# Keeping split tiles and split weights in DRAM between two attention layers

## The chip, the cores and the metric

The kernel runs on one core of one Trainium2 chip. A core has five engines that run side by side and meet through semaphores: TensorE (PE, matmuls), VectorE (DVE), ScalarE (ACT), GpSimd (POOL) and SyncE (SP). SP does no arithmetic here: it issues the transfers (DMAs) between DRAM and the core's own memory, in the order of its instructions. If one of them has to wait, all behind it wait too. The metric is the device time of one execution in microseconds (us). Less is better.

## What is computed

The input `x` has 2048 rows (positions) of 640 numbers, in float32. Four layers follow one another, each with a layer normalization ahead of it and added to its own input:

```
x = x + A(layernorm(x), wqkv, wo)                 # attention
x = x + B(layernorm(x), dft_seq, dft_hid)         # FNet mixing
x = x + A(layernorm(x), wqkv, wo)                 # the same weights again
x = x + B(layernorm(x), dft_seq, dft_hid)         # the same matrices again

A: qkv = x @ wqkv; 32 heads of 20; each position attends to 8 positions,
   itself and those 2, 4, ... 14 before it; softmax; result @ wo
B: a = x @ dft_hid_re.T;  b = x @ dft_hid_im.T
   y = dft_seq_re @ a - dft_seq_im @ b
```

Both attention layers use the same `wqkv`, and both FNet layers the same sequence matrices. What is prepared from them in one layer can therefore be used in another.

## The kernel before

A float32 product is made of three matmuls in a reduced format. An operand is split into a high part (a rounded copy, made by ACT) and a low part (what is left, a subtraction made by DVE or POOL). The matmuls are high by high, high by low and low by high (`PASSES`, L210). "Split" means this pair from here on. A split tile takes twice the room of the raw one.

The work is four calls: `layer_a(0)`, the FNet layer `b1`, `layer_a(2)`, the FNet layer `b2`.

**The attention layers** (`layer_a`) follow a list written out by hand. The function `at(step, phase, ...)` puts a call into a step, from −7 to 66, and a phase of that step; the phases of a step run in the order of `PHASES` (L806), among them `dma` near the beginning and `dmaw`, `dmas`, `misc`, `dmac`, `dmar` near the end. Every engine, SP included, gets its instructions in that order. The work has three strands:

- PE makes the query, key and value products (`qkv_mm`, L344, 64 groups of 15 matmuls). Quarter `q` of the heads uses the split weights `wq[q]`, which live in the buffer `r1_q`. ACT copies each group out, and SP stores it to DRAM (`kvb`, `qb`).
- DVE and POOL do the attention itself, in 32 units of two half steps. SP loads a unit's queries (`q_load`) and its windows of keys and values (`w_load`, L399, in five buffers `win`). DVE multiplies (L423, L461), POOL and DVE sum (L425, L431, L476 to L478), ACT does the exponential (L439) and copies the queries (L396).
- PE makes the output product (`wo_mm`, L501) and, in the last third (steps 49 to 66 and a tail), already begins the FNet layer: `z_mm` (L916) multiplies the normalized rows by the first of eight sequence tiles, in 16 pieces `s` of 128 by 512. These pieces are the tile c0.

In the first attention layer c0 comes raw: `c_load` (L881) loads a piece, `c_hi` (L885) and `c_lo` (L900) split it into a buffer `ct[s]`. In the second, `c_get` (L890) loads a piece that is already split, from the DRAM buffer `c0b`, into the same three (at the end four) buffers in turn:

```
tag = ("s3", "s0", "s2", "s1")[s % (3 if s < 12 else 4)]
```

**The FNet layers** (`LayerB`) take the other sequence tiles in pairs (`pair`, L1091). PE's order in them is written by hand; for the other engines a scheduler orders the instructions by a simulated timeline. A pair has three loops over eight pieces; in the second one (L1159 to L1173), in the first FNet layer and for pairs 0 and 1 alone, the line

```
if self.li == 1 and p < 2:
    self.c_keep(p * NP + i, views, tags)
```

loads one more raw piece of c0, splits it and stores both parts to `c0b`. This is how `c0b` is filled before the second attention layer reads it. The products of `zt` with the DFT weights, which lead to `y`, are at L994 (`ymm`). They come at fixed places of each pair and serve as marks in time.

**The join.** The last pair of the first FNet layer runs inside `early()` (L565) of the second attention layer, with hooks that begin the attention layer's transposes. At hook 7 `w0` loads and splits the weights of quarter 0; quarters 1 to 3 follow after the pair. `a_weights_q` (L204) does this for five pieces of a quarter: a raw piece into a `win` buffer, then ACT (L123) and DVE (L127) split it into `r1_q`. In the first attention layer the weights are split elsewhere (`wq_split`, L540), in the first few steps.

## Time and profile before

| | us |
|---|---|
| runs shown (three): median | 1813.44 |
| lowest and highest | 1812.18, 1818.15 |
| the profiled execution | 1810.4 |
| its span, first to last instruction | 1808.5 |
| PE busy, of the span | 1746.1 |
| mean granted TensorE clock | 0.992 |

The rows of the profile give an engine's busy time, the number and the mean length of a group of instructions, and behind a bar how long the engine stood idle ahead of them and what ended that. "L354" is line 354 of the kernel. PEld is the loading of weights into TensorE, which runs beside the matmuls. A row of the order in time has the start and the length in us. "SPq" marks an instruction of SP that issues a DMA; the name `win<-kvb` means that `win` is written from `kvb`. A matmul's end is modelled, so a PE that is shown busy may still be short of its peak. In the windows view, each row is a stretch of the span, with the busy time of PE, PEld, DVE, ACT and POOL, then the granted clock, the mean busy share of the 16 DMA engines, and the rate in GB/s.

### The profile page before, as it was taken

The page shows a single profiled execution, that of the slowest core. Times are in us where ns is not written, and L with a number is a line of the kernel's source. Part 1 is how long each engine was busy: PE and PEld are TensorE (multiplying, and loading weights), DVE is VectorE, ACT ScalarE, POOL GpSimd, SP SyncE. Part 2 cuts the span into 40 slices and gives each one's busy share as a digit, 9 for nine tenths or more (in the row PEclk, how much of TensorE's full clock was granted, in tenths as well). Part 3 has the DMA queues.
Part 4 walks back from the last instruction along what each step waited for, and adds up shares of the span by engine and source line. Part 5 has one row for each costly group of instructions (what it writes and reads, how often), then busy time and mean ns, then how long its engine had stood idle before and what let it go on. Part 6 is the DMA issues. An engine that isn't in the chain of part 4 may idle for free.

```text
span 1808.5 us, 26471 instructions
## 1 busy us (share of the span) xinstructions
PE 1746.1 (97%) x8798; PEld 1508.9 (83%) x8798; DVE 1380.1 (76%) x2129; ACT 818.9 (45%) x1708; POOL 640.6 (35%) x597
## 2 busy tenths in 40 slices
PE   9999997989999999999999999999899999999999
PEld 6879886777887887888888889877788888888888
DVE  5899899888768767767739988887777677676673
ACT  5544544544445445445533334444434443443441
POOL 3799898960000000000008987899400000000000
PEclk9999998999999999999999999999999999999999
DMA  6776667647789689677647856687687766876761
GB/s 233 224 263 208 208 203 247 218 164 280 273 267 332 223 270 336 221 258 229 215 132 226 278 181 199 200 296 261 218 295 257 259 226 225 265 231 223 259 210 52
DMA packets 273738, 423.59 MB, mean 234 GB/s; under 512 B 22688, under 2 KB 152736, under 8 KB 273344
## 3 DMA queue, kind: packets, MB, share of 16 engines
q1 hardware_dynamic: 270400, 419.92, 70.0%
q10 hardware_dynamic: 3200, 1.97, 0.4%
q8 instruction: 70, 1.15, 0.2%
q14 instruction: 68, 0.56, 0.1%
HBM read 336.66 MB, written 85.14 MB: 233 GB/s over the span
## 4 chain that ended last, share of the span: by engine, by line
PE 65%; DVE 12%; DMA 10%; POOL 6%; ACT 3%; issue 3%; SPq 1%; DVEq 0%; ACTq 0%; POOLq 0%
PE m L354 17%; PE aux L994 13%; PE t L1083 9%; PE m L1083 9%; PE xt L1083 4%; PE pq L1083 4%; PE aux L501 4%; DMA win<-cs_in 2%; DVE pr L423 2%; DVE pr L461 2%; PE m L916 2%; PE t L916 2%; POOL pr L476 2%; DMA c0b<-r 2%; DVE r L1077 1%
## 5 line engine op out<-in xcount | busy, mean ns | idle before, releaser
L354 PE MATMUL m<-r,s 128*128 128x480 f32 x1920 | 439.9, 384 | 5.7 <-ACT s L224 2.4
L354 PEld LDWEIGHTS m<-r,s 128*128 128x128 f32 x1920 | 357.5, 189 | 61.5 <-ACT s L224 3.8
L166 POOL TENSOR_TENSOR stats<-stats,mhalf 128x1 f32<-128x1 f32 (+1 forms) x40 | 30.4, 761 | 564.9 <-ACT stats L162 564.8
L1076 ACT CAST r<-win 128x512 fp32r<-128x512 f32 x244 | 149.4, 620 | 178.4 <-DVE win L1112 75.5
L994 PE MATMUL aux<-r2a,zo 128*128 128x320 f32 x768 | 226.5, 310 | 0.0
L476 POOL TENSOR_TENSOR pr<-pr 128x640 f32<-128x640 f32 x126 | 200.9, 1595 | 40.7 <-DVE pr L461 39.7
L423 DVE TENSOR_TENSOR pr<-pq,win 128x1280 f32<-128x1280 f32 x128 | 189.8, 1483 | 29.9 <-ACT pq L396 29.3
L994 PE MATMUL aux<-pr,zo 128*128 128x320 f32 x704 | 208.2, 308 | 0.0
L1077 DVE TENSOR_TENSOR r<-win,r 128x512 fp32r<-128x512 f32 x244 | 164.5, 686 | 46.8 <-ACT r L1076 40.7
L461 DVE TENSOR_TENSOR pr<-pq,win 128x1280 f32<-128x1280 f32 x128 | 190.8, 1491 | 4.5 <-DVE pq L456 0.2
L425 POOL TENSOR_TENSOR pr<-pr 128x640 f32<-128x640 f32 x128 | 183.4, 1433 | 18.7 <-DVE pr L423 15.6
L1083 PE MATMUL m<-r,r 128*128 128x512 f32 x600 | 154.7, 392 | 0.4 <-DVE r L1077 0.4
L994 PEld LDWEIGHTS aux<-r2a,zo 128*128 128x128 f32 x768 | 144.1, 188 | 2.0
L1083 PE MATMUL t<-r,r 128*128 128x512 f32 x498 | 135.4, 393 | 2.5 <-issue 2.5
L916 PE MATMUL m<-s,r 128*128 128x512 f32 x384 | 119.8, 399 | 15.3 <-DMA s<-c0b 6.7
L1083 PEld LDWEIGHTS m<-r,r 128*128 128x128 f32 x600 | 112.4, 188 | 25.8 <-DVE r L1077 0.7
L994 PEld LDWEIGHTS aux<-pr,zo 128*128 128x128 f32 x704 | 132.1, 188 | 2.0
L916 PE MATMUL t<-s,r 128*128 128x512 f32 x384 | 118.4, 395 | 2.3 <-DVE ot L976 1.5
L361 ACT COPY stg<-m 128x480 f32<-128x480 f32 x128 | 70.9, 556 | 104.6 <-PE m L354 94.0
L477 POOL TENSOR_TENSOR pr<-pr 128x320 f32<-128x320 f32 x126 | 114.4, 908 | 9.9
L431 DVE TENSOR_REDUCE lg<-pr 128x64 f32<-128x640 f32 x128 | 103.9, 811 | 17.7 <-POOL pr L425 17.4
L1083 PEld LDWEIGHTS t<-r,r 128*128 128x128 f32 x498 | 93.4, 188 | 24.6 <-issue 3.3
(269 smaller groups left out, 3246.3 us busy)
## 6 DMA issues: line engine op xcount, KB each, us to landing
win<-cs_in SPq DMA_DIRECT2D x358, 256.0 KB, 4.1
r<-xc SPq DMA_DIRECT2D x240, 256.0 KB, 4.3
win<-kvb SPq DMA_DIRECT2D x96, 440.0 KB, 4.8
xa<-cs_in SPq DMA_DIRECT2D x124, 256.0 KB, 4.2
win<-kvb SPq DMA_DIRECT2D x64, 360.0 KB, 5.3
xc<-stg SPq DMA_DIRECT2D x40, 512.0 KB, 3.1
kvb<-stg SPq DMA_DIRECT2D x60, 320.0 KB, 3.9
xr<-xs SPq DMA_DIRECT2D x40, 320.0 KB, 3.2
```

The source lines that it names most:

```text
L354: nc.tensor.matmul(mt[g][:, : 3 * F], st[:, a, k], wq[q][:, b, k], start=n == 0, stop=n == 14)
L423: nc.vector.tensor_tensor(pr, q, wview(u, jp, 0, [[1, FE]]), op=ALU.mult)
L425: nc.gpsimd.tensor_tensor(pv[:, :, 0:10], pv[:, :, 0:10], pv[:, :, 10:20], op=ALU.add)
L431: nc.vector.tensor_reduce(lgs[u][:, 2 * jp : 2 * jp + 2].rearrange("p j w h -> p (j w h)"), prq.pop((u, jp))[:, :, 0:10], axis=AX.X, op=AL ...
L461: nc.vector.tensor_tensor(pr.rearrange("p j w (h d) -> p j w h d", d=DH), lgs[u][:, 2 * jp : 2 * jp + 2].unsqueeze(4).to_broadcast([P, 2, ...
L476: g.tensor_tensor(pr[:, :, 0:4], pr[:, :, 0:4], pr[:, :, 4:8], op=ALU.add)
L477: g.tensor_tensor(pr[:, :, 0:2], pr[:, :, 0:2], pr[:, :, 2:4], op=ALU.add)
L916: self.last = nc.tensor.matmul(self.z[t][k], self.xn[c][:, a, j, k * P : (k + 1) * P], self.ct[s][:, b], start=s == 0 and i == 0, stop=s = ...
L994: self.last = nc.tensor.matmul(self.ym[e][:, :320], zt[(k, a, ri)][:, j2 * P : (j2 + 1) * P], w[:, e * 320 : (e + 1) * 320], start=(k, a, ...
L1076: nc.scalar.copy(hi, raw)
L1077: nc.vector.tensor_tensor(lo, raw, hi.bitcast(F32), op=ALU.subtract)
L1083: nc.tensor.matmul(bank, w(a, kb), hl[b], start=start and (a, b) == (0, 0), stop=stop and (a, b) == (1, 0),)
```

## The change

The first attention layer now stores what it has split anyway. `wq_keep` writes the split weights of quarter `q`, piece `k`, to a new DRAM buffer `wqb`, at step 16 + 4k + q, in the phase `dmar`. `c_keep` now writes `ct[s]` to `c0b` straight from the buffer that the products read, in the step of the piece's first product; pieces 14 and 15 are written in the tail. The FNet layer's `c_keep` calls are gone.

The second attention layer loads the split weights with `wq_get` into `r1_q`: quarter 0 at hook 7, quarter 1 after the pair, quarters 2 and 3 from the list, at steps −5 to −3 and −2 to 0. `a_weights_q` is gone, and with it twenty splits. Its pieces of c0 now go through five buffers: `s3`, `s2`, the two `stg` buffers and `s0`. The first five are loaded in steps 48 to 50, the others one step after the last product of the piece that held the buffer, though no later than the step before their own first product. In the first attention layer the buffers' turn is `s3`, `s2`, `s0` in place of `s3`, `s0`, `s2`.

```diff
+    wqb = dr.tile([P, NQ, KD, 2, 3 * F], F32, name="wqb")
...
-    def a_weights_q(q):
-        wt = T([P, 2, KD, 3 * F], f"r1_{q}", F32R)
-        for k in range(KD):
-            split(wt[:, 0, k], wt[:, 1, k], wq_load1(q, k))
-        return wt
...
+        def wq_keep(q, k):
+            nc.sync.dma_start(wqb[:, q, k], wq[q][:, :, k].bitcast(F32))
+
+        def wq_get(q, k):
+            if k == 0:
+                wq_begin(q)
+            nc.sync.dma_start(wq[q][:, :, k].bitcast(F32), wqb[:, q, k])
...
             def w0():
                 with tc.issue_after(prev.dma.ins):
-                    wq[0] = a_weights_q(0)
+                    for k in range(KD):
+                        wq_get(0, k)
...
-            for q in range(1, NQ):
-                wq[q] = a_weights_q(q)
+            for k in range(KD):
+                wq_get(1, k)
+                at(-5 + k // 2, "dmar", wq_get, 2, k)
+                at(-2 + k // 2, "dmar", wq_get, 3, k)
...
+            for q in range(NQ if first else 0):
+                at(16 + NQ * k + q, "dmar", wq_keep, q, k)
...
                 at(t - 1, "misc", handoff.c_lo, z)
+                at(t, "dmac", handoff.c_keep, z)
+            elif z < 5:
+                at(*((48, "dma"), (48, "dma"), (48, "dmac"), (49, "dma2"), (50, "dmac"))[z], handoff.c_get, z)
             else:
-                at(t - 1, "dmac", handoff.c_get, z)
+                at(max(50, min(thirds[3 * z - 13] + 1, t - 1)), "dma2", handoff.c_get, z)
...
+            at(64, "dmac", handoff.c_keep, 13)
...
                 handoff.c_hl(14)
+                handoff.c_keep(14)
...
                 handoff.c_hl(15)
+                handoff.c_keep(15)
...
-            tag = ("s3", "s0")[s % 2] if t else ("s3", "s0", "s2", "s1")[s % (3 if s < 12 else 4)]
+            tag = ("s3", "s0")[s % 2] if t else ("s3", "s2", "s0", "s1")[s % (3 if s < 12 else 4)]
...
         def c_get(self, s):
-            tag = ("s3", "s0", "s2", "s1")[s % (3 if s < 12 else 4)]
-            self.ct[s] = T([P, 2, 512], tag, F32R)
+            tag = ("s3", "s2", "stg", "stg", "s0")[s % 5]
+            self.ct[s] = T([P, 2, 512], tag, F32R, bufs=2 if tag == "stg" else 1)
             nc.sync.dma_start(self.ct[s].bitcast(F32), c0b[:, s])
 
-        def c_keep(self, s, views, tags):
-            hi, lo = self.s_split(self.s_raw(0, s, tags), views)
-            for a, v in enumerate((hi, lo)):
-                nc.sync.dma_start(c0b[:, s, a].rearrange("p (r t) -> p r t", r=2), v.bitcast(F32))
+        def c_keep(self, s):
+            nc.sync.dma_start(c0b[:, s], self.ct[s].bitcast(F32))
...
-                    if self.li == 1 and p < 2:
-                        self.c_keep(p * NP + i, views, tags)
```

## The prediction

> **What bounds the kernel now.** I read the page first, then windows of engine time by stage, then the waits and single engines in order of time around each place that the diff touches.
>
> ```profile
> span 1808.5 us, 26471 instructions
> PE 1746.1 (97%) x8798; PEld 1508.9 (83%) x8798; DVE 1380.1 (76%) x2129; ACT 818.9 (45%) x1708; POOL 640.6 (35%) x597
> ```
>
> TensorE (PE) is busy for 1746 of 1808 us and no matmul is added or removed, so only its 62 us of idle time, and time at a lowered clock, can be won. The question is which of it the change reaches. The next answer is the windows view (us; busy time of PE, weight load, DVE, ACT, POOL; granted clock; DMA share; GB/s). The windows are four passes of the same code in `pair`: from the first y product of a pair to the second. The chain and the order of time give their bounds (the chain dates a matmul 0.16 us later, at both ends alike).
>
> ```profile
> 520.98 8.82 PE aux L994 x60
> 572.25 8.82 PE aux L994 x60
> 659.25 0.30 PE L994 MATMUL aux<-r2a,zo 128*128 128x320 f32 x1
> ...
> 520.82:572.09 51.27, 48.87 (x229) 40.11 (x228) 33.92 (x54) 24.47 (x44) 0.00 (x0) 1.00 0.93 327
> 659.25:712.40 53.15, 50.23 (x230) 41.30 (x228) 33.42 (x55) 24.95 (x45) 0.00 (x0) 0.97 0.91 316
> 799.55:847.02 47.47, 47.47 (x230) 40.37 (x228) 31.23 (x49) 21.11 (x39) 0.00 (x0) 1.00 0.68 223
> 1416.78:1464.25 47.47, 47.47 (x229) 40.37 (x228) 30.02 (x48) 19.65 (x34) 0.00 (x0) 1.00 0.75 245
> ```
>
> Pairs 0 and 1 of the first FNet layer hold the sixteen old `c_keep` calls (L1173); pair 2 and the second FNet layer have none. Without them the stage takes 47.47 us with PE never idle; with them 51.27 and 53.15. Who waits is in the answers on the line that stores (L898):
>
> ```profile
> L898 SPq DMA_DIRECT2D c0b<-r x22: 359/377/513, 536.2 to 711.8; - x22
> L898 SPq DMA_DIRECT2D c0b<-s x10: 319/327/636, 521.5 to 694.7; - x10
>   ACT r L1076: 12.6, 5
>   ACT s L1076: 7.3, 2
>   DVE r L1077: 5.0, 1
> DMA to landing us min/median/max: 4.5/5.3/6.2
> ```
>
> 32 stores of 256 KB each hold a split buffer for 4.5 to 6.2 us, and ACT and DVE stand still for 24.9 us until stores let go. DMA engines are at 0.91 to 0.93 there, against 0.68 to 0.75 without.
>
> **The change part by part.**
>
> *Pairs 0 and 1 lose the keep.* Sixteen extra loads (256 KB), 32 stores, 16 ACT and 16 DVE splits go. The price is the window difference: (51.27 − 47.47) + (53.15 − 47.47) = 3.80 + 5.68 = 9.48 us. PE is in order and its idle time is gone at 47.47, so what is late next is PE itself, and everything after moves up. Ends: 0 (something else as long turns up) and −9.48. I take −9.5, for two undisturbed passes lie at 47.47 exactly.
>
> *The join into the second attention layer.* Twenty raw weight loads with 20 ACT and 20 DVE splits become twenty loads of split pairs (480 KB).
>
> ```profile
> L123 ACT ACTIVATE r<-win 128x480 fp32r<-128x480 f32 x20 | 11.9, 603 | 4.6 <-DMA win<-wqkv_in 3.5 <-PE m L1083 0.8
> L127 DVE TENSOR_TENSOR r<-win,r 128x480 fp32r<-128x480 f32 x20 | 12.8, 655 | 5.9 <-ACT r L123 5.8
> 875.00:940.00 65.00, 62.87 (x369) 57.74 (x368) 30.94 (x57) 29.49 (x61) 0.00 (x0) 1.00 0.47 147
> 876.26 5.01 SPq L201 DMA_DIRECT2D win<-wqkv_in  x5
> 892.02 1.60 ACT L123 ACTIVATE r<-win 128x480 fp32r<-128x480 f32 x3 [0.78 <-PE m L1083]
> 893.82 3.94 PE L354 MATMUL m<-r,s 128*128 128x480 f32 x17
> 914.70 0.71 PE L354 MATMUL m<-r,s 128*128 128x480 f32 x2 [1.28 <-ACT s L224]
> 916.30 3.09 PE L354 MATMUL m<-r,s 128*128 128x480 f32 x13 [0.57 <-ACT s L224]
> 928.18 3.23 PE m L354 x15
> ```
>
> The splits take 11.9 us of ACT and 12.8 of DVE, but PE idles only 65.00 − 62.87 = 2.13 us in the stretch. The 1.28 us wait for ACT's transposed copy (L224), queued behind splits and statistics, should go; the 0.57 is the turn PE to ACT to PE and mostly stays. I take −1.5. Ends: −2.1 (all idle time), and above if the loads are late. At the stage's 327 GB/s for a share of 0.93, full engines move about 352 GB/s, so 480 KB take 1.4 us. The five loads of quarter 0 are issued near 876 and the first product is at 893.8: five times 1.4 and the 5.3 of a landing end near 888, 5 us early. Quarter 1 needs buffer r1_1, free at about 892 (the row of ACT waiting for PE); ten loads for quarters 1 and 2 are 14 us, in by 911; the first product of quarter 1 is at 928. Quarter 3 is put on SP behind the first attention loads:
>
> ```profile
> 943.53 0.43 SPq L409 DMA_DIRECT2D win<-kvb  x1
> 948.40 1.48 DVE L423 TENSOR_TENSOR pr<-pq,win 128x1280 f32<-128x1280 f32 x1
> win<-kvb SPq DMA_DIRECT2D x96, 440.0 KB, 4.8
> ```
>
> That window has 4.87 us from issue to use and lands in 4.8; two quarter-3 loads ahead of it (2.8 us, issued some 2 us earlier) make it about 1 us late. DVE's next steps wait for PE's evacuations anyway, so I count 0 and keep +1 as the end.
>
> *Tile loads of the second attention layer: five buffers, started earlier.*
>
> ```profile
> PE m L916 <- DMA s<-c0b: 6.7, 4, 2.7
> 1184.00:1287.00 103.00, 91.68 (x484) 78.44 (x484) 88.25 (x135) 44.29 (x112) 97.67 (x90) 0.98 0.81 276
> L476 POOL TENSOR_TENSOR pr<-pr 128x640 f32<-128x640 f32 x19 | 29.8, 1571 | 2.3 <-DVE pr L461 2.3
> 1286.19 0.66 POOL L478 TENSOR_TENSOR zo<-pr 128x160 f32<-128x160 f32 x1
> 1287.64 0.60 PE L319 MATMUL pq<-ident,zo 128*128 128x128 f32 x4
> ```
>
> The waits on c0b are 6.7 us in four places, but POOL is busy for 97.67 of these 103 us. Its last sum ends at 1286.85; the last transposes start at 1287.64, behind it and DVE's sibling sums. A PE that never waits for tiles would wait there instead. Only POOL's 2.3 us of waiting for DVE can move, where DVE waited for a late PE. I take −0.3; ends −2.3 and +1 (2.5 MB of tiles bunched in two steps at a DMA share of 0.81).
>
> *First attention layer: twenty weight stores of 480 KB, steps 16 to 35.*
>
> ```profile
> 119.00:222.00 103.00, 103.00 (x544) 91.86 (x543) 93.18 (x131) 56.58 (x148) 93.67 (x91) 1.00 0.66 210
> 167.21 0.42 SPq L409 DMA_DIRECT2D win<-kvb  x1
> 175.83 1.48 DVE L423 TENSOR_TENSOR pr<-pq,win 128x1280 f32<-128x1280 f32 x1
> ```
>
> 9.8 MB in 103 us are 95 GB/s more: 305 of 352, share 0.66 to about 0.9. They wait for nothing, having been split long before, and SP's issue is some 0.4 us each. Behind them stand the window loads; the pair shown has 8.6 us from issue to use, over 4.8 to land: a store ahead costs 1.4 of 3.8 spare. I take +0.2; ends 0 and +3 (single misses). The Trainium skill, in DMA: Bandwidth & Descriptors, section Bandwidth, measures 425 GB/s for large loads by a core alone and sets about 358 where HBM binds. By the first figure the queue would be at 0.72 and this part free; the trace's 352 says the second, with a sum 0.2 us higher.
>
> *First attention layer's tail: sixteen tile stores of 512 KB, steps 49 to the end, and slots in another order.*
>
> ```profile
> 272.00:387.00 115.00, 97.36 (x493) 83.88 (x491) 103.76 (x155) 53.31 (x128) 105.79 (x94) 0.93 0.68 224
> ACT s L888 <- DMA stg<-cs_in: 17.3, 8, 3.6
> 327.14 0.62 ACT L888 CAST s<-stg 128x512 fp32r<-128x512 f32 x1 [2.31 <-DMA stg<-cs_in]
> 331.10 1.49 DVE L423 TENSOR_TENSOR pr<-pq,win 128x1280 f32<-128x1280 f32 x1 [0.22 <-ACT pq L396]
> 433.18 0.83 DVE L125 SCALAR_TENSOR_TENSOR zo<-xa,zo 128x640 fp32r<-128x640 f32 x1 [0.63 <-ACT zo L123]
> ```
>
> DVE and POOL are busy 104 and 106 of 115 us, so every delay to them counts. A keep waits on SP for DVE's low part of the step before, where SP already waits for windows that DVE frees; behind it in the queue are the raw tile loads, for which ACT waits in order (17.3 us in eight places), and behind ACT the softmax and the query copies. 512 KB at 352 GB/s are 1.5 us. At 327 the delay shows: ACT waits 2.31 us for a tile, and DVE 0.22 for the query copy behind it. I count that place in full (1.5) and half a microsecond for the rest, since elsewhere ACT mostly waits for DVE: +2.0, ends 0 and +6. The last two keeps share the queue with the next layer's DFT weights, whose last split ends at 434.0, just when it is used: +0.3, ends 0 and +2.
>
> Sum: −9.5 − 1.5 − 0.3 + 0.2 + 2.0 + 0.3 = −8.8 us, on the profiled 1810.4 us (span 1808.5): 1801.6. The median of the runs shown, 1813.4, is 3.0 above that profile; against it the sum is about 1804.6. I say 1804.
>
> **Rivals.**
>
> *The tile waits were worth their full time.* If the end of the second attention layer follows PE, 6.7 us go, and the 2.3 above are not the limit: 1804 − 6.4 = 1798. For it: the chain passes through c0b loads. Against: POOL is full.
>
> *The join gives the gain back.* Split loads are twice as large and must wait for the weight buffer itself, where raw tiles waited in window buffers. If quarter 0's loads, on a queue with more ahead of them than I count, lose the 5 us by which they are early and, say, another landing and a load (5.3 + 1.4, some 7 us), PE stands at the first product: 1804 + 7 = 1811. Against: share 0.47.
>
> *Slower: the store queue stalls the first tail.* ACT meets a raw tile 1.5 us late for each of 13 tiles, and nothing absorbs it: 13 × 1.5 = 19.5 in place of 2.0, so 1804 + 17.5 = 1821. The other terms win 10.8 us, so the kernel is slower than before from the eighth uncovered tile on, and by over 0.3% from the eleventh. Against: in the row of that line ACT waits for eight tiles only, and DVE is behind it in one of the rows. A second way to the same stall is the slot, now held until the store has landed (5.3 us), but its next tile comes three tiles later. The Trainium skill, DMA: Bandwidth & Descriptors, section Anatomy of one DMA, says completion waits for the write receipt, HBM's the heaviest, and puts 2.0 us plus bytes over 436 GB/s on a DMA; that would be 3.2 us for 512 KB. The 5.3 measured for half the size speaks for the queue as the larger part.
>
> **How the numbers follow.** Forecast with its terms' ends: 0.72, for its main term stands in two pairs of windows. Full tile waits 0.06, join 0.13, slower 0.09. A change of 0.3% (5.4 us) is about what a measurement of this kernel can tell from none: faster is below 1808.0. So faster 0.78, same 0.13, slower 0.09. The range takes in the forecast's ends and the join, and leaves out the slow case: 1797 to 1811; the likeliest case alone has 1797 to 1808.
>
> **What would show it.** Both stages at 47.5 us with a DMA share near 0.7 and no c0b store; the join without the 1.28 us wait; no c0b waits of PE at the second tail, but POOL's last sum as late after the layer's start as now, and a new short wait of PE for it; in the first tail ACT's waits for raw tiles grown from 17.3 us and that stretch 2 us longer. Wrong would be a first tail longer by over 8 us, PE idle ahead of the first product of the second attention layer, or windows landing after DVE wants them in steps 16 to 35.

## The result, and the profile after

| | us |
|---|---|
| the changed kernel: median of four runs | 1827.2 (1824.6 to 1830.2) |
| the kernel before, beside it on the same chip | 1815.0 (1812.2 to 1818.2) |
| ratio, with its 95% interval | 1.0071 (1.0056 to 1.0086) |
| profiled execution after, its span | 1827.6, 1825.8 |

The change made the kernel slower by 0.7%, some 12 us; the forecast was 1804. In all comparisons below, the runs of the kernel before lay between 1810.3 and 1820.8 us, so its profile (1810.4) is one of its quickest executions. Differences between the two profiles (17.3 us of span) are therefore some 5 us larger than those between medians. Places and waits are read from the profiles, verdicts from the runs.

The head of the page after:

```profile
span 1825.8 us, 26342 instructions
PE 1755.1 (96%) x8798; PEld 1519.0 (83%) x8798; DVE 1371.7 (75%) x2093; ACT 800.8 (44%) x1672; POOL 641.1 (35%) x597
```

ACT and DVE have less to do (800.8 against 818.9, 1371.7 against 1380.1), as the splits are gone, and yet the span is longer. The windows view of the changed kernel shows where (columns as in the prediction: the stretch, busy time of PE, PEld, DVE, ACT, POOL, granted clock, DMA share, GB/s):

```profile
119.00:222.00 103.00, 103.00 (x543) 91.77 (x543) 93.08 (x131) 56.91 (x148) 93.61 (x91) 1.00 0.92 300
272.00:387.00 115.00, 92.28 (x473) 79.52 (x471) 103.56 (x146) 49.63 (x119) 101.65 (x90) 0.93 0.81 271
532.65:580.12 47.47, 47.47 (x230) 40.37 (x229) 30.05 (x48) 21.39 (x39) 0.00 (x0) 1.00 0.75 242
667.43:714.89 47.46, 47.46 (x229) 40.36 (x228) 31.60 (x50) 22.96 (x42) 0.00 (x0) 1.00 0.77 250
1187.00:1298.00 111.00, 96.32 (x485) 84.25 (x484) 94.50 (x137) 44.75 (x113) 97.87 (x90) 0.91 0.75 260
1298.00:1341.00 43.00, 36.31 (x154) 29.61 (x154) 33.19 (x57) 22.47 (x46) 1.74 (x2) 0.88 0.75 255
```

and the same view of the kernel before, for the stretch from its last attention sum (1287.0) to the first y product of the second FNet layer:

```profile
1287.00:1323.00 36.00, 33.05 (x159) 26.86 (x158) 24.76 (x45) 19.26 (x40) 1.10 (x2) 1.00 0.62 210
```

- Pairs 0 and 1 take 47.47 and 47.46 us, from 51.27 and 53.15: the main term of the forecast, to the tenth.
- Steps 16 to 35 (first row) lose nothing with twenty weight stores at a DMA share of 0.92.
- The first attention layer's tail is slower: in the same 115 us PE gets 92.3 us of work done in place of 97.4, POOL 101.7 in place of 105.8. The last attention sum ends at 399.4 instead of 392.7, and the y mark of pair 0 is at 532.6 instead of 520.8.
- The second attention layer's tail needs 111 us for what took 103, and the join into the next layer 43 for what took 36. The sum there ends 11.0 us late, the first y product is 18.1 late. From there on the changed kernel stays 16 to 18 us behind.

**First tail.** ACT's waits for raw tiles in 272 to 387, and the landing times of three transfers in 272 to 400 (KB each, median us from issue to landing), after:

```profile
ACT s L902 <- DMA stg<-cs_in: 30.7, 8, 6.9
...
win<-kvb SPq DMA_DIRECT2D x31, 360.0 KB, 5.7
c0b<-s SPq DMA_DIRECT2D x14, 512.0 KB, 4.8
stg<-cs_in SPq DMA_DIRECT2D x14, 256.0 KB, 5.3
```

and before:

```profile
win<-kvb SPq DMA_DIRECT2D x31, 360.0 KB, 3.8
stg<-cs_in SPq DMA_DIRECT2D x14, 256.0 KB, 3.0
```

In the median a raw tile lands 2.3 us later, with the stores in the same queue, and ACT's 17.3 us of waiting for raw tiles have become 30.7. These 13.4 us are not the loss: in the same stretch ACT waits 12.6 us less for VectorE ahead of the exponential (30.5 before, 17.9 after). The loss is the 6.7 us at the last sum.

**Second tail.** VectorE's instructions in order of time, after (start, length, and in brackets the idle time ahead with what ended it):

```profile
1272.94 1.51 DVE L1051 TENSOR_TENSOR s<-r 128x1024 f32<-128x1024 f32 x1 [1.36 <-PE aux L496]
1274.37 1.48 DVE L456 TENSOR_TENSOR pr<-pq,win 128x1280 f32<-128x1280 f32 x1
...
1282.15 2.08 DVE L1051 TENSOR_TENSOR s<-r 128x1024 f32<-128x1024 f32 x1
...
1290.94 2.03 DVE L1059 TENSOR_TENSOR stg<-s,s 128x512 f32<-128x512 f32 x1
...
1294.30 1.48 DVE L456 TENSOR_TENSOR pr<-pq,win 128x1280 f32<-128x1280 f32 x1
1295.70 0.68 DVE L1061 TENSOR_TENSOR stg<-stg 128x512 fp32r<-128x512 f32 x1
...
1297.67 0.33 DVE L473 TENSOR_TENSOR zo<-pr 128x160 f32<-128x160 f32 x1
```

L456 and L473 are the attention's last products and sums. L1051, L1059 and L1061 are not attention: they are `x_whole` and `x_combine` of the *next* FNet layer (L1039, L1047 and L1049 of the kernel before). The kernel before ran the first of them 17 us behind its last sum:

```profile
1304.43 1.22 DVE L1039 TENSOR_TENSOR s<-r 128x1024 f32<-128x1024 f32 x1
```

Now they stand in VectorE's queue ahead of the last attention steps and cost 1.36 + 1.51 + 2.08 + 2.03 + 0.68 = 7.7 us. Behind the last sum the moved work costs more. ACT's copy for `x_combine` (L1060) waits for VectorE's L1059 and stands ahead of ACT's copy of the last transposes (L318), for which PE's output product waits. After:

```profile
1299.80 0.62 ACT L1060 CAST stg<-stg 128x512 fp32r<-128x512 f32 x1 [5.41 <-DVE stg L1059]
1300.33 0.64 ACT L318 CAST zo<-pq 128x256 fp32r<-128x256 f32 x2
1300.75 3.07 PE L496 MATMUL aux<-r2a,zo 128*128 128x320 f32 x12 [1.81 <-ACT zo L318]
1310.10 0.82 DVE L128 TENSOR_TENSOR r2a<-xa,r2a 128x640 fp32r<-128x640 f32 x1
1310.94 0.33 SPq L188 DMA_DIRECT2D xa<-wim_in  x1
```

and before:

```profile
1288.70 2.18 PE L501 MATMUL aux<-r2a,zo 128*128 128x320 f32 x12 [0.46 <-ACT zo L323]
1296.47 0.82 DVE L127 TENSOR_TENSOR r2a<-xa,r2a 128x640 fp32r<-128x640 f32 x1
1297.31 0.33 SPq L187 DMA_DIRECT2D xa<-wim_in  x1
```

PE waits 1.81 us in place of 0.46, and this product and the next take 3.07 and 3.09 us in place of 2.18 and 2.36: 3.0 us more. The first DFT weights are split into `r2a`, which holds the output weights until these products end, and the second weights are loaded into `xa` once VectorE has split the first (L128). So that load is issued 13.6 us later than before, 2.6 more than the sum is late. ACT waits for the weights in order, and PE for the tile that ACT splits behind them, after:

```profile
1320.21 0.74 ACT L124 ACTIVATE r2a<-xa 128x640 fp32r<-128x640 f32 x1 [2.25 <-DMA xa<-wre_in]
...
1322.97 0.79 PE L928 MATMUL m<-s,r 128*128 128x512 f32 x1 [3.73 <-ACT s L902]
```

Why is the next layer's work there? Its order is not written by hand: a scheduler puts each instruction where a simulated timeline finds its buffers free. `x_whole` writes into `s1` and `s2`. In the kernel before, the last pieces of c0 (14 and 15) held these two buffers to the very end. The new `c_get` never uses `s1`, and `s2` for the last time at piece 11. So the sums become "ready" in the middle of the tail. The new turn in the first attention layer does the same on a smaller scale: `s2` is held by piece 13 and no longer by 14, and the next layer's first sum starts 11.5 us behind the last attention sum, where it was 15.9 before.

**Start of the second attention layer.** VectorE's waits in 930 to 985, after, and SP's order there:

```profile
DVE pr L418 <- DMA win<-kvb: 5.3, 2, 3.5
```

```profile
941.86 0.98 SPq L544 DMA_DIRECT2D r<-wqb  x2
943.86 0.33 SPq L388 DMA_DIRECT2D qs<-qb  x1
944.23 0.43 SPq L404 DMA_DIRECT2D win<-kvb  x1
944.71 0.43 SPq L544 DMA_DIRECT2D r<-wqb  x1
```

Windows land after DVE wants them, since weight loads of quarter 3 are ahead of them. The ninth attention step begins 36.7 us after the first, against 33.9.

### The profile page after: what moved, and what is told of

It is laid out like the page before. It is cut to its first block, busy times and chain, and to the rows that moved or that the text cites. A ratio compares the mean times of both kernels' runs of the same rounds, so it can differ in the third digit from the quotient of the medians.

```text
span 1825.8 us, 26342 instructions
## 1 busy us (share of the span) xinstructions
PE 1755.1 (96%) x8798; PEld 1519.0 (83%) x8798; DVE 1371.7 (75%) x2093; ACT 800.8 (44%) x1672; POOL 641.1 (35%) x597
## 4 chain that ended last, share of the span: by engine, by line
PE 74%; DVE 11%; DMA 6%; POOL 4%; ACT 3%; issue 3%; SPq 0%; DVEq 0%; ACTq 0%; POOLq 0%
PE m L349 16%; PE aux L1006 15%; PE t L1095 11%; PE m L1095 11%; PE pq L1095 5%; PE xt L1095 5%; PE aux L496 4%; DVE pr L418 3%; DVE pr L456 2%; PE m L928 2%; PE t L928 2%; DMA stg<-cs_in 1%; DMA win<-kvb 1%; POOL pr L471 1%; POOL pr L420 1%
## 5 line engine op out<-in xcount | busy, mean ns | idle before, releaser
L456 DVE TENSOR_TENSOR pr<-pq,win 128x1280 f32<-128x1280 f32 x128 | 190.9, 1491 | 4.5 <-DVE pq L451 0.2
L928 PE MATMUL m<-s,r 128*128 128x512 f32 x348 | 111.3, 409 | 15.0 <-ACT r L877 5.0
L928 PE MATMUL t<-s,r 128*128 128x512 f32 x348 | 107.8, 399 | 0.9 <-DVE ot L988 0.9
```

Source lines behind the costliest of these rows:

```text
L456: nc.vector.tensor_tensor(pr.rearrange("p j w (h d) -> p j w h d", d=DH), lgs[u][:, 2 * jp : 2 * jp + 2].unsqueeze(4).to_broadcast([P, 2, ...
L928: self.last = nc.tensor.matmul(self.z[t][k], self.xn[c][:, a, j, k * P : (k + 1) * P], self.ct[s][:, b], start=s == 0 and i == 0, stop=s = ...
```

## The experiments

Each kernel was timed beside the kernel before; a ratio is against it. Four marks are used, in us of the profile: the end of the first attention layer's last sum (392.7 before, 399.4 after), the y mark of pair 0 (520.8, 532.6), the end of the second layer's last sum (1287.0, 1298.0), and the first y product of the second FNet layer (1322.8, 1340.9).

"Back" below is the difference of two medians. Taken from the ratios, the same differences come out up to 2.4 us larger (12.3 as 13.2, 10.8 as 11.4, 4.1 as 6.5, 3.8 as 5.8, 2.0 as 2.5), so none of them is good to better than a microsecond or two.

### The buffers at the end of the second tail

```diff
-            tag = ("s3", "s2", "stg", "stg", "s0")[s % 5]
+            tag = ("s3", "s2", "stg", "stg", "s0")[s % 5] if s < 14 else ("s2", "s1")[s - 14]
```

> The changed kernel with one edit: in the second attention layer pieces 14 and 15 of c0 go through the buffers s2 and s1, as pieces 14 and 15 did in the kernel before; pieces 0 to 13 keep the five buffers and their early loads. Theory (the next layer's work moved up): with s1 and s2 free early, the scheduler put the next FNet layer's first whole-tile sums and combinations into VectorE's queue among the last attention steps. With s1 and s2 held to the end they go back behind the last sum: the last attention sum, 11.0 us late against the kernel before, comes back to about 3.5 late, the first y product of the second FNet layer from 18.1 late to 4 to 6 late, and the time falls by 10 to 14 us. Rival (bunched tile loads in steps 48 to 50): the loads are unchanged, so the time stays within 1.5 us of the changed kernel.

Measured: 1814.9 us, ratio 0.9998 (0.9986 to 1.0010): 12.3 us back from two buffer names. The last sum ends at 1290.9, the first y product comes at 1327.4. VectorE's order there:

```profile
1290.41 0.53 DVE L473 TENSOR_TENSOR zo<-pr 128x160 f32<-128x160 f32 x1
...
1309.05 1.22 DVE L1051 TENSOR_TENSOR s<-r 128x1024 f32<-128x1024 f32 x1
```

The next layer's first sum is behind the last attention sum again. All bunched loads are still there, so they are not the cause.

```diff
-            tag = ("s3", "s2", "stg", "stg", "s0")[s % 5]
+            tag = ("s3", "s0", "s2", "s1")[s % (3 if s < 12 else 4)]
...
-                at(max(50, min(thirds[3 * z - 13] + 1, t - 1)), "dma2", handoff.c_get, z)
+                at(t - 1, "dmac", handoff.c_get, z)
```

> The changed kernel with the second attention layer's tile loads as before: buffers s3, s0, s2 and at the end s1, each loaded in the step ahead of its first product. Both theories of the second tail expect the 11 to 14 us back (the moved-up work goes, and so do the bunched loads), with TensorE's waits of about 6.7 us for tiles of c0 there again. If early loads are worth something apart from that, this one is slower than the run with pinned buffers by up to 2.3 us; if the bunched loads cost, faster by as much as they cost. If the second tail's loss comes from neither, the time stays near the changed kernel's 1827.

Measured: 1815.0 us, ratio 0.9992 (0.9979 to 1.0005), the same as with five buffers and early loads. PE waits for tiles of c0 again, where the run before has no such wait:

```profile
PE m L926 <- DMA s<-c0b: 4.2, 3, 2.6
```

Taken by itself, what the five buffers were to give is not measurable: the end of the tail follows POOL and DVE, not the tile loads.

### The turn of the buffers in the first tail

```diff
-            tag = ("s3", "s0")[s % 2] if t else ("s3", "s2", "s0", "s1")[s % (3 if s < 12 else 4)]
+            tag = ("s3", "s0")[s % 2] if t else ("s3", "s0", "s2", "s1")[s % (3 if s < 12 else 4)]
```

> The changed kernel with the first attention layer's buffers in the old turn (s3, s0, s2, then s1). All stores stay. Theory (the stores cost the first tail and the next layer's start, 6.7 and about 5 us): the turn of the buffers decides only when s2 comes free for the next layer's sums, so up to 4 us may come back, all behind the last attention sum, and the sum itself stays about 6.7 late. Rival (the new turn made the tail slow): the last sum comes back to within 2 us of the kernel before and the time falls by 6 us or more.

Measured: 1823.5 us, ratio 1.0039 (1.0025 to 1.0052), 3.8 us back. The last sum stays at 399.4; the y mark of pair 0 comes to 530.8. As the first theory has it, the turn matters only for the work behind the sum: the next layer's first sum goes back to 17.5 us behind it. The marks place 1.8 us there; the rest comes up later, in places that the edit does not touch, and is not explained.

> The changed kernel with both edits on the buffers: pieces 14 and 15 through s2 and s1 in the second attention layer, and the old turn (s3, s0, s2) in the first. If the two single effects, 12.3 and 3.8 us, are apart, the time is about 1811, some 4 us under the kernel before; if they share a cause, 1814 to 1815.

The edits are those of the first and the third run together. Measured: 1812.7 us, ratio 0.9984 (0.9974 to 0.9993). The time lies between the two that were expected. Together the two edits give 14.6 us of their 16.1, and the kernel is a shade faster than the one before, with all the stores in place.

### The tile stores

```diff
-                at(t, "dmac", handoff.c_keep, z)
...
-            nc.sync.dma_start(self.ct[s].bitcast(F32), c0b[:, s])
+            nc.sync.dma_start(
+                self.ct[s].bitcast(F32).rearrange("p a (r t) -> p a r t", r=2),
+                xcb[0][list(XC)[s // 4]][:, 2 * (s % 4) : 2 * (s % 4) + 2],
+            )
```

> The changed kernel without the sixteen tile stores of the first attention layer; the second attention layer's tile loads read as many bytes from another buffer instead (the combined rows of the first FNet layer), so the products of c0 there are not those of the reference. The turn of the buffers stays the new one. Theory (stores, by their place in the queue or their traffic): the last attention sum of the first layer, 6.7 us late, comes back to within 1 us of the kernel before, and the second y mark of the FNet layer, 11.8 late, to within 2; the time falls by 9 to 12 us. Rival (the turn of the buffers): 3 us or less.

Measured: 1816.4 us, ratio 1.0008 (0.9997 to 1.0020), 10.8 us under the changed kernel. The last sum is at 393.3 and the y mark at 523.1, just over the 2 us expected. So the sixteen stores cost 10.8 us, by the marks 6.1 at the last sum and 3.4 more by the y mark. (The second layer's tile loads read another buffer here, so a part of the last microsecond may be theirs.)

To see how, the stores were moved behind the raw loads of their step:

```diff
-                at(t, "dmac", handoff.c_keep, z)
+                nxt = thirds[3 * z + 9] - 2 if z < 10 else t + 1
+                at(min(t + 1, nxt), "dmar", handoff.c_keep, z)
```

> The changed kernel with the tile stores of the first attention layer moved back in SP's queue: up to a step later and behind the raw tile loads of their step, as far as the buffer's next use allows; pieces 14 and 15 stay. As many bytes are stored. Theory (the raw loads land late because a 512 KB store stands directly ahead of them): ScalarE's waits for raw tiles in the tail, 30.7 us against 17.3 before the change, come back to about 20, the last attention sum from 6.7 late to 2 to 4 late, and the time falls by 3 to 5 us. Rival (the bytes load the DMA engines wherever they stand, or the stores hold the buffers): the last sum stays 5 to 8 late and the time within 1.5 us of the changed kernel.

Measured: 1823.1 us, ratio 1.0035 (1.0024 to 1.0047), 4.1 us back; the last sum is at 396.2, 3.5 late. ACT's waits in 300 to 400 of this kernel show what is left:

```profile
ACT s L903 <- DMA c0b<-s: 17.5, 6, 5.0
ACT s L903 <- DMA stg<-cs_in: 12.5, 4, 4.9
```

The copy into a tile buffer waits, in six places, for the store that still reads that buffer. No instruction of the changed kernel waits for a store in this way; the later place brings this wait in. To separate it from the mere bytes, the stores took the same bytes from another tile:

```diff
-                at(min(t + 1, nxt), "dmar", handoff.c_keep, z)
+                at(min(t + 1, nxt), "dmar", c_keep_other, z)
...
+        def c_keep_other(z):
+            nc.sync.dma_start(c0b[:, z], wo_s["w"][:, :, z % KD, 0:512].bitcast(F32))
```

> The kernel with the tile stores moved behind the raw loads, but pieces 0 to 13 are stored from another tile of the same size (the split output weights, which stay in place to the layer's end), so that as many bytes leave in the same places and no piece's own buffer has to wait for its store. What the second attention layer then reads as c0 is not c0. Theory (what is left of the first tail's loss, 3.5 us at the last attention sum, is the buffer held until its store has landed): ScalarE no longer waits for stores, and the last sum is at most 1 us later than in the kernel before; the time falls by 2 to 3 us against the run with late stores. Rival (traffic): the last sum stays 3 us or more late.

Measured: 1818.6 us, ratio 1.0017 (1.0008 to 1.0026), 4.5 us under the run before it. The last sum is at 393.3, 0.6 late, and in the same stretch ACT waits for raw tiles alone:

```profile
ACT s L906 <- DMA stg<-cs_in: 17.8, 7, 5.2
```

The raw loads of 272 to 400, in the run with late stores and in this one:

```profile
stg<-cs_in SPq DMA_DIRECT2D x14, 256.0 KB, 5.0
```

```profile
stg<-cs_in SPq DMA_DIRECT2D x14, 256.0 KB, 3.5
```

So the bytes cost almost nothing at the last sum; what costs is where the stores stand and who waits for them. How the 6.1 us divide is not shown. In the changed kernel the wait that grew is the one for raw tiles. The late stores trade a part of it for waits for the buffer, worth 2.9 us at the sum, and even there raw tiles land late, so that a store directly ahead of them is not the whole of it.

### The weights

```diff
                 wq_get(1, k)
-                at(-5 + k // 2, "dmar", wq_get, 2, k)
-                at(-2 + k // 2, "dmar", wq_get, 3, k)
+            for k in range(KD):
+                wq_get(2, k)
+                at(-5 + k // 2, "dmar", wq_get, 3, k)
```

> The changed kernel with the split weights of quarter 2 loaded right behind those of quarter 1 and quarter 3 in the steps where quarter 2 was, three steps earlier. Theory (the five loads of quarter 3 stand ahead of the first attention windows): VectorE's waits for windows at the layer's start, 5.3 us in two places, go; the ninth attention step, 36.7 us behind the first against 33.9 in the kernel before, comes back to 34 to 35; the time falls by 2 to 3 us. Rival (the layer's start is late for another reason, or the loads now delay the first queries): within 1 us of the changed kernel.

Measured: 1825.2 us, ratio 1.0057 (1.0041 to 1.0073), 2.0 us back. The waits for windows are gone, and the ninth step begins 34.0 us after the first, so the mechanism is shown; its worth in time is less sure, since the two intervals overlap.

The next kernel is the one before with `wqb`, `wq_keep` and `wq_get` as in the change, and nothing else of it.

> The kernel before with the weights' part of the change alone: twenty stores of split weights in the first attention layer, twenty loads in place of raw loads and splits at the join; the tiles stay as before. By the prediction's terms (stores +0.2, join -1.5) the time is 1.3 us under the kernel before. By what the changed kernel's trace shows (join -1.8, but windows late by 2 to 3 us at the start of the second attention layer) it is 0.5 to 1.5 us above it. In the first attention layer every attention step starts within 0.3 us of the kernel before by both.

Measured: 1812.4 us, ratio 0.9988 (0.9979 to 0.9998). The prediction's terms are borne out, and my correction of them from the changed kernel's trace is not, although the window waits are there (the ninth step is 35.8 behind the first). A likely reason: the profile of the kernel before was a quick execution, so that what is read against it looks late.

> The kernel before with the weights' part alone, and quarters 2 and 3 loaded earlier. Against the weights' part alone (0.9988 of the kernel before): 2 to 3 us less, as in the changed kernel, so about 1810, ratio 0.997. If the second tail's end follows GpSimd alone, whatever the start does, equal to it.

With the edit above: 1810.1 us, ratio 0.9973 (0.9962 to 0.9983), some 2 us less again, with intervals that again overlap.

### Spreading what the pairs did

If the second loop of a pair is too full, the old work could be spread. In the old `c_keep` scheme, once with the early weights above and once on the kernel before as it is:

```diff
+            def keep(here):
+                if self.li == 1 and p < 2 and here:
+                    self.c_keep(self.nkeep, views, tags)
+                    self.nkeep += 1
...
                     self.product(m7, x7, c7, *ends)
+                    keep(i in (2, 5))
...
-                    if self.li == 1 and p < 2:
-                        self.c_keep(p * NP + i, views, tags)
+                    keep(i in (1, 3, 6))
...
                     self.product(m6, x6, c6, *ends)
+                    keep(i in (1, 3, 5))
```

> The kernel before with the weights' part, quarters 2 and 3 early (1810 us), and the sixteen pieces of c0 loaded, split and stored in pairs 0 and 1 as before, but spread over all three loops of a pair (2, 3 and 3 pieces) in place of eight in the second loop. Theory (the 9.5 us that the tiles cost in the pairs come from eight of them standing in one of three loops): 5 to 9 us of the 9.5 come back, 1802 to 1806, under both kernels and under the run with the four edits. Rival (each piece costs 0.6 us wherever it stands): 1809 to 1811.

> The kernel before with the spreading alone: nothing else of the change. By the first theory of the spread run the two pairs, 51.3 and 53.2 us in the kernel before, come to 47.5 to 49.5 each, and the time is 4 to 9 us under the kernel before; by its rival the pairs stay at 51 to 53 and the time within 1 us.

Measured: 1821.2 us (ratio 1.0031, 1.0018 to 1.0043) and 1821.5 (1.0031, 1.0020 to 1.0043). None of the expectations held: the theory had both kernels faster, the rivals had them about where they were, and they are some 6 us slower than the kernel before. The pairs of the second run, in windows:

```profile
521.90:577.20 55.30, 50.42 (x230) 41.17 (x229) 35.84 (x57) 25.59 (x48) 0.00 (x0) 0.97 0.82 267
664.40:719.20 54.80, 50.28 (x229) 41.33 (x228) 34.95 (x57) 23.86 (x45) 0.00 (x0) 0.95 0.80 265
```

They take 55.3 and 54.8 us, at a DMA share of 0.8 and not 0.92. ACT and DVE still wait 23.4 us for the stores to let go of a split buffer (24.9 before), and a store still lands in 5.1 us (5.3). A lower share with longer pairs speaks against full DMA engines as the price; how it comes about in the other loops I did not settle.

### Putting the mends together

> The changed kernel with four edits together: pieces 14 and 15 through s2 and s1 in the second attention layer, the old turn of the buffers in the first, tile stores behind the raw loads, quarters 2 and 3 of the weights loaded earlier. If the single effects (16.1 us for both buffer edits, 4 for the stores, 2 for the weights, less what measured 14.6 together for the first two) add, about 1807, 8 us under the kernel before (ratio 0.995 to 0.996). Rival (what is saved ahead of the second attention layer's tail is waited for there, behind GpSimd): 1810 to 1813.

The edits are those shown above: buffers `s2` and `s1` for pieces 14 and 15, the old turn, the late stores, the early weights. Measured: 1808.3 us, ratio 0.9965 (0.9952 to 0.9978), 7.9 us under the kernel before (1816.2 beside it) and near the 1807 expected.

```diff
-            nc.sync.dma_start(c0b[:, s], self.ct[s].bitcast(F32))
+            nc.scalar.dma_start(c0b[:, s], self.ct[s].bitcast(F32))
```

> The kernel with the four edits, with the sixteen tile stores issued by ScalarE, on its own queue, at the same places of the list. Theory (what is left of the stores' cost is their place ahead of loads in SP's queue): 1 to 4 us under the run with the four edits, if ScalarE's waits for VectorE's low parts cost nothing. Rival (what is left is traffic, or ScalarE then stands still for the low parts and holds up the softmax): equal, or slower by up to 6 us.

Measured: 1810.0 us, ratio 0.9969 (0.9957 to 0.9981): no gain. The Trainium skill, DMA: Bandwidth & Descriptors, section "Issuing engines are not separate DMA queues", says that transfers from different engines run on the same 16 DMA engines, and that another issuer saves only the time to issue; this run agrees.

Two ways to store earlier, so that the buffer is free again in time, in place of the late stores:

```diff
-                at(t, "dmac", handoff.c_keep, z)
+                at(t - 1, "dmar", handoff.c_keep, z)
```

> The kernel with the four edits, but the tile stores at the end of the step in which the low part is made (one to two steps earlier than in the run with the four edits, and behind the raw loads of that step). Theory (the buffer held until its store has landed is what is left, 3.5 us): the store lands before the buffer's next turn, ScalarE's waits for stores go, the last attention sum comes within 1.5 us of the kernel before, and the time falls by 2 to 4 us against the four edits (1808.3), to 1804 to 1806. Rival (SP now stands still for the low part, with the next step's windows behind it): equal or slower by up to 5 us.

```diff
-                at(t, "dmac", handoff.c_keep, z)
+                at(t, "dma", handoff.c_keep, z)
```

> The same, with the tile stores at the head of the next step, when the low part is surely there: ahead of that step's window and raw loads. Theory as for the run with early stores: the last sum within 2 us of the kernel before, 1804 to 1807. If the raw loads behind the stores are late again (as in the changed kernel), the waits for raw tiles are above 25 us and the time 1809 to 1812.

Measured: 1809.8 us (0.9963, 0.9952 to 0.9974) with the last sum at 395.8, later than expected, and 1807.6 us (0.9955, 0.9939 to 0.9971) with it at 393.8, as expected, though the time is just above the 1804 to 1807. The intervals overlap, so the two are not told apart by time. ACT's waits in 272 to 400, in the run with late stores and in the second of these two:

```profile
ACT s L904 <- DMA c0b<-s: 18.3, 6, 5.3
ACT s L904 <- DMA stg<-cs_in: 15.9, 6, 5.6
```

```profile
ACT s L903 <- DMA stg<-cs_in: 23.3, 10, 4.1
```

The earlier store takes the wait for the buffer away and brings 7.4 us of waiting for raw tiles back. The last sum, at 397.3 with late stores, gains 3.5 us all the same.

That leaves the last two pieces. First one in each of pairs 0 and 1, on the kernel with late stores:

```diff
-                handoff.c_keep(14)
...
-                handoff.c_keep(15)
...
+                    if self.li == 1 and p < 2 and i == 4:
+                        self.c_keep_pair(14 + p, views, tags)
```

> The kernel with the four edits, but pieces 14 and 15 of c0 are not stored in the first attention layer's tail: they are loaded, split and stored once more in pairs 0 and 1 of the first FNet layer, one in each, as in the kernel before. Theory (the last two stores stand ahead of the next layer's DFT weights and windows, and cost some 3 to 4 us at the start of the FNet layer; in a pair each costs 9.5/16 = 0.6): 2 to 3 us under the run with the four edits. Rival (the start of the FNet layer is late for another reason): within 1 us of it.

Measured: 1811.4 us, ratio 0.9976 (0.9966 to 0.9986), where 2 to 3 us under that kernel were expected and none came. The y mark comes from 531.2 to 525.0, but pair 1 takes 49.9 us in place of 47.5. Then both in pair 0 (`p == 0 and i in (2, 5)`), on the kernel with stores at the head of the step:

> The kernel of the run with stores at the head of the step, but pieces 14 and 15 are not stored behind the last attention sums: they are loaded, split and stored again in pair 0 of the first FNet layer, at its third and sixth place. Theory (what is late between the first layer's last sum, 1.1 us late, and the y mark of the first pair, 5.6 late, is the two last stores ahead of the DFT weights): that mark is 2 to 3 us late at most, the pair costs 0.5 to 1.5 more, and the time falls by 2 to 3 us, to 1804 to 1806. Rival (another cause there, or the pair takes back what the start wins): 1807 to 1809.

Measured: 1806.6 us, ratio 0.9950 (0.9934 to 0.9965), just above the 1804 to 1806. The y mark is at 522.9, against 526.4 with the stores in the tail. The two pairs in windows:

```profile
522.86:570.86 48.00, 47.92 (x229) 40.18 (x229) 29.81 (x47) 21.15 (x39) 0.00 (x0) 1.00 0.83 275
658.10:705.60 47.50, 47.50 (x230) 40.40 (x229) 30.26 (x48) 21.46 (x40) 0.00 (x0) 1.00 0.74 235
```

The mark moved as expected, for 0.5 us in the pair. By the runs the step from 0.9955 to 0.9950 is within both intervals, so its worth stays open. This kernel has the lowest ratio of all: 0.5% under the kernel before and, by the two ratios, 1.2% under the changed one.

## Why the prediction was wrong

- **Pairs, −9.5: right.** 47.47 and 47.46 us are what the undisturbed passes showed.
- **Weight stores, +0.2: right.** The share is 0.92 where "about 0.9" was said, and attention steps start no more than 0.3 us later than in the kernel before up to step 52.
- **The join, −1.5: right; its window end, counted 0, was worth about 2.** The y products of the join come back from 2.5 to 0.7 us late, 1.8 won. But the windows behind quarter 3's loads were late by 5.3 us in two waits, not by 1, and moving the loads gave 2.0 us. "DVE's next steps wait for PE's evacuations anyway" was the wrong cover.
- **Five buffers, −0.3 with ends −2.3 and +1: this step failed.** What it said of the tail's bound is nearly right: POOL decides, together with VectorE, whose last sum ended 0.2 us behind POOL's, and the five buffers alone change nothing that can be measured. But it let only "POOL's 2.3 us of waiting for DVE" move: it treated the buffers as something only the tile loads use, and took VectorE's order as given. The buffers' release moved the next layer's sums up into VectorE's queue, ahead of the last attention steps: 12.3 us, far outside both ends.
- **Tile stores and slot order, +2.0 with ends 0 and +6: the direction was right, the size was not.** ACT did wait for raw tiles (17.3 to 30.7 us), each landing 2.3 us later where 1.5 was taken, and more than one place was uncovered. All sixteen stores together cost 10.8 us, where the sum has 2.3. The hold of the buffer, set aside among the rivals with "but its next tile comes three tiles later", was indeed no wait of the changed kernel; it came with the later stores, as in steps 56 to 58 the buffer's next copy stands only one step behind the tile's first product. The slot order had no price in the sum; it cost 3.8 us.
- **The last two stores, +0.3 with ends 0 and +2: too small by the marks.** Without them the y mark of pair 0 is 3.5 us earlier with the stores at the head of the step, and 6.2 with late stores (1.0 of it at the last sum already), while the runs do not separate the kernels.
- **The rivals.** The slower one, with 0.09, named both ways in which stores hurt, but its 19.5 us came from thirteen uncovered tiles; the stores alone, at 10.8, would have left the kernel about where it was (−9.5 − 1.8 + 2.0 + 10.8 = +1.5). The mechanism that made it slower was in no rival. The 3.2 us that this rival takes from the Trainium skill (DMA: Bandwidth & Descriptors, section Anatomy of one DMA) come from a fit for transfers that GpSimd issues; here SP issues them, and 512 KB landed in 4.8 us in the median.
- **The signs of being wrong: none of the three came.** The first tail was longer by 6.7 us and not over 8, PE did not idle ahead of the second attention layer's first product, and no window was late in steps 16 to 35. None had been set for the second tail, where most of the time went. What was to show the forecast there did not come: POOL's last sum ends 851 us behind the layer's first attention product, and not 844 as before.

The measured effects are not a closed sum: −9.5 − 1.8 + 2.0 + 0.2 + 12.3 + 10.8 + 3.8 = +17.8 us, against some 12 measured. The two edits of the buffers already gave less together than one by one; the rest of the difference is open.

With the side effects mended, and two pieces left in a pair, the change brings about what was forecast: the ratio of 0.9950 is 9 us, where the sum said 8.8. That the two are so close is partly luck, since this kernel also has weight loads and stores in places that the sum did not price.

## What to carry to other kernels

A buffer's name is also a date: where a scheduler orders later work by free buffers, releasing one early can pull that work into the queue of the engine that is the bound. Before giving a tile another buffer, look up who takes that buffer next and on which engine. A store can cost far more than its bytes: these sixteen, counted as little more than one transfer's time, cost 10.8 us. Where it stands decides who pays. Ahead of the raw loads it was the raw tiles; behind them it was the buffer's next user, which waited until the store had landed.

## What was unexpected in the hardware

The same VectorE instruction takes up to three times as long beside POOL. VectorE's `x_combine` twice, and POOL's row at the first of them, after:

```profile
1290.94 2.03 DVE L1059 TENSOR_TENSOR stg<-s,s 128x512 f32<-128x512 f32 x1
...
1304.27 0.69 DVE L1059 TENSOR_TENSOR stg<-s,s 128x512 f32<-128x512 f32 x1
```

```profile
1290.89 1.54 POOL L471 TENSOR_TENSOR pr<-pr 128x640 f32<-128x640 f32 x1 [1.20 <-DVE pr L456]
```

POOL begins 0.05 us earlier and ends at 1292.43; VectorE then needs 0.54 us more. Later, with POOL idle, it needs 0.69 in all. The Trainium skill, SBUF — State Buffer, section "SBUF: two separate sides", calls the port pair of the two engines an exclusive lock, which a VectorE instruction with two operands in that memory loses for the whole of a POOL instruction that began first. The rows agree to 0.15 us, and this made the moved-up work dearer than its length behind the tail.

A long wait also slows what follows it on PE. After a wait of 4.04 us, eighteen matmuls of the output product took 4.42 us; the same eighteen in the kernel before took 2.90. PE's rows, after and before:

```profile
1288.41 1.22 PE L928 MATMUL m<-stg,r 128*128 128x512 f32 x2 [4.04 <-DVE r L880]
...
1294.06 4.42 PE L496 MATMUL aux<-r2a,zo 128*128 128x320 f32 x18 [1.10 <-ACT zo L337]
```

```profile
1284.89 2.90 PE L501 MATMUL aux<-r2a,zo 128*128 128x320 f32 x18 [0.19 <-ACT zo L342]
```

The granted clock agrees: it was 0.50 in the 2.6 us behind the wait and 0.61 during the eighteen matmuls, against 1.00 during the same eighteen before. Each of PE's five waits of over 3.7 us in the changed kernel (4.12, 4.98, 3.85, 4.04 and 3.73) was followed by 2.5 us at 0.50. After shorter waits the clock differed: 1.00 behind one of 2.33 us in the kernel before, 0.50 behind one of 2.76.
